# Moving accumulating DMAs of block sums, and operands at a pair's border, in an attention and feed-forward kernel

## The chip, the cores and the metric

The kernel runs on one core of a Trainium2 chip. The core has a matrix engine (TensorE, in the profile PE, with its weight loads as PEld), a vector engine (VectorE, DVE), a scalar engine (ScalarE, ACT) and GpSimd (POOL). SyncE (SP), ScalarE and GpSimd issue DMAs from queues of their own. Each engine works through its instructions in the order in which they were planned. The metric is the time of one execution on the device in microseconds (us); lower is better.

## The reference, cut to what matters

Attention within chunks of 64 tokens, whose result is the input of a feed-forward network with a leaky activation:

```python
scores = scale * np.matmul(q_c, k_c.transpose(0, 1, 2, 4, 3))      # 8 batches, 8 heads, chunks of 64, head size 64
scores = scores - np.max(scores, axis=-1, keepdims=True)
attn = np.exp(scores)
attn = attn / (np.sum(attn, axis=-1, keepdims=True) + 1e-09)
x = np.matmul(attn, v_c)                    # 4608 tokens x 512, once the heads are side by side
h = x @ w_in                                # 512 x 2048
g = np.maximum(h, 0.0) + alpha * np.minimum(h, 0.0)
out = g @ w_out                             # 2048 x 512
```

All is float32. The kernel keeps that precision on TensorE by splitting each operand into a high and a low part (`hi`, `lo`) and adding three products: high by high, low by high and high by low.

## The kernel before

The 4608 tokens are 36 pieces of 128 (`NSUB`) and 9 blocks of 512. The first three blocks (`PLAIN`) go through the network directly. The other six go in three pairs; a pair's two products are done by a scheme with seven half-size products in place of eight (`ORDERS` holds the order of the seven), for which combinations of weights are needed.

**The plain blocks.** There are 48 steps (`n`, from 0). Step `n` takes 128 of the 2048 hidden features (`f`) of one block: an input product of 12 matmuls into a bank of `ps_h` (`ffn_in`, L318), PReLU on ScalarE and VectorE (`prelu`, L308 to L310), a split (L330, L331), and an output product of 12 matmuls into the four banks `ps_o` (`ffn_out`, L343). The output product comes one step later, and from step 20 on two steps later (`pending`). Blocks 0 and 1 are done in two turns each (`phases`, `TURNS`), since the weights are still arriving: features 0 to 2 of block 0, 0 to 8 of block 1, then the rest of each, then all of block 2. After a first turn `store` copies the four banks to SBUF and stores them in DRAM tiles `partial` (L375). After the second turn it copies them to `more` (rows 0 and 1, one tile with one buffer), to `ob` (row 2) and to `g` (row 3) at L372, and adds each in DRAM to its `partial` with an accumulating DMA from GpSimd's queue (L377). Block 0's second turn ends in step 26 and block 1's in step 33. SyncE moves the sums from `partial` to the output in step 47 (L774).

**Combinations of weights.** In the sixteen steps of `COMBINE` (20, 22, 23, 24, 26, 29, 30, 31, 33, 35, 36, 37, 39, 40, 41, 43) `combine` takes a pair of weight tiles, forms sums and differences on VectorE (L499 to L509), splits two results with a cast on ScalarE (L515) and a subtraction on VectorE (L516), and stores each in two halves from GpSimd's queue (L477). The split tiles are buffers of a stage pool: `raw` has two buffers, `more` one. With `early`, only `raw` is used; otherwise the three take turns.

**Attention beside it.** From step 21 on, pieces of attention are done by visits between the matmuls (`visit`, at the half steps of `visits`): values of an older piece (L279) and scores of a new one (L201) into two banks `ps_a`, then maxima on VectorE (L217), exponentials on ScalarE (L221), sums and a transposition (L223 to L232, eight small DMAs at L239), and copies of the older piece's result (L295, L304, L305). The next visit uses the same two banks. Since `pinned` is set from step 20 on, TensorE's order is the program's; the other engines' orders are written by a planner that simulates the kernel in time and goes by priorities (`high_priority`, offset 300) and by `issue_after`, which puts an instruction behind another one on the same engine.

**The pairs.** A pair has eight rounds of `first_product` (L598: input products and PReLU, with tiles `gh`, `g` and `gl` of two buffers each), and then `second_product` (L714): seven products of eight operands each, numbered 0 to 55 (`at`), each six matmuls long. An operand is split by `operand` (L554 and L555), two operands ahead of its use (`AHEAD`), into tiles that go by `at % 4`: 0 into the two buffers `t1`, 1 into `more`, 2 and 3 into `gh` and `gl`. The combined weights stream in from GpSimd's queue (L536). At the end of the last pair `add` adds the last two banks to `y21` (L676), and `done` stores the two results from SyncE's queue (L685).

Of the kernel before, what the change touches and what calls it, by code (L numbers as in the profile page):

```python
# [27 lines left out]
def tile_local_attention_prelu_ffn(  # L28
# [12 lines left out]
    nc = tc.nc  # L41
# [31 lines left out]
    def f32(t):  # L73
        return t.bitcast(F32)
# [272 lines left out]

    partial = {}
    finals = []

    def store(acc, b, keep):
        for t, o in enumerate(acc):
            rows = slice(b * TB + t * P, b * TB + (t + 1) * P)
            before = partial.get((b, t))
            if b == PLAIN - 1:
                ob = const.tile([P, DM], F32, name=f"wi{NF - 2 - t}")
            elif keep and b == 0:
                side = "wi" if t % 2 else "wo"
                ob = const.tile([P, DM], F32, name=f"{side}{NF - 1 - t // 2}")
            elif keep:  # L360
                pool, name = ((load, "q_sb"), (load, "v_sb"), (load, "v_sb"), (soft, "pr"))[t]
                ob = pool.tile([P, DM], F32, name=name, bufs=2 if name == "v_sb" else 1)
            elif t < 2:
                if t == 0:
                    both = stage.tile([P, 2, DM], F32, name="more", bufs=1)
                ob = both[:, t]
            elif t == 2:
                ob = stage.tile([P, DM], F32, name="ob", bufs=1)
            else:
                ob = gp.tile([P, DM], F32, name="g")  # L370
            with tc.high_priority(offset=HIGH):
                nc.scalar.copy(ob, o)  # L372
            if keep:
                partial[b, t] = dram.tile([P, DM], F32, name=f"partial{b}_{t}")
                nc.sync.dma_start(out=partial[b, t], in_=ob)  # L375
            elif before is not None:
                nc.gpsimd.dma_start(out=before, in_=ob, accum_op=ALU.add)  # L377
                finals.append((out[rows, :], before))
            else:
                nc.sync.dma_start(out=out[rows, :], in_=ob)  # L380
# [93 lines left out]

    def keep_a(side, i, j, a):
        n, u = unit(side, i, j)
        nc.gpsimd.dma_start(out=units[side][n][:, u], in_=f32(a))  # L477

    halves = (slice(0, 2 * P), slice(2 * P, 4 * P))

# [10 lines left out]
    def combine(side, j, early):  # L491

        ws = wi if side == "wi" else wo
        pair = [ws[j], ws[JF + j]]
        left, right = halves
        a = []
        for w in pair:
            t = stage.tile([P, 512], F32, name="t1")
            nc.vector.tensor_tensor(t, f32(w[:, 0]), f32(w[:, 1]), op=ALU.add)  # L499
            a.append(t)  # L500
        a11, a22 = a[0][:, left], a[1][:, right]
        if side == "wi":
            a12, a21 = a[0][:, right], a[1][:, left]
        else:
            a21, a12 = a[0][:, right], a[1][:, left]
        nc.vector.tensor_tensor(a22, a21, a22, op=ALU.add)
        nc.vector.tensor_tensor(a21, a11, a21, op=ALU.subtract)
        nc.vector.tensor_tensor(a11, a22, a11, op=ALU.subtract)
        nc.vector.tensor_tensor(a12, a12, a11, op=ALU.subtract)  # L509
        names = ((2, 4), (3, 1)) if side == "wi" else ((2, 3), (4, 1))  # L510
        for t, name in zip(a, names):
            which = "raw" if early else ("raw", "raw", "more")[fetched[0] % 3]
            fetched[0] += 1
            w = stage.tile([P, 2, 512], F32R, name=which, bufs=2 if which == "raw" else 1)
            nc.scalar.copy(w[:, 0], t)  # L515
            nc.vector.tensor_tensor(w[:, 1], t, f32(w[:, 0]), op=ALU.subtract)  # L516
            for half, s in zip((left, right), name):
                keep_a(side, {1: 5, 2: 6, 3: 7, 4: 3}[s], j, w[:, :, half])

    sequence = [(side, n) for _ in range(NPAIR) for side in ("wi", "wo") for n in range(7 * JF // 2)]  # L520
    ring = []
# [130 lines left out]
    def operand(g, at):  # L652
        i, j = ORDERS["wo"][at // JF], at % JF
        b11, b12, b21, b22 = pieces(g, j)
        if i == 7:
            t = gp.tile([P, TB], F32, name="g")
            with tc.issue_after(behind[0][1].ins):
                nc.vector.tensor_tensor(t, b22, b12, op=ALU.subtract)
        else:
            t = {1: b11, 3: b22, 2: b21}.get(i, b12)  # L660
        if at % 4 == 1:
            both = stage.tile([P, 2, TB], F32R, name="more", bufs=1)
            hi, lo = both[:, 0], both[:, 1]
        else:
            pool, names = (stage, ("t1", "t1")) if at % 4 == 0 else (gp, ("gh", "gl"))
            hi, lo = (pool.tile([P, TB], F32R, name=name) for name in names)
        behind[:] = behind[1:] + [split(t, hi, lo)]
        return hi, lo

    def second_product(g, b, operands, conversion, end):  # L670
# [3 lines left out]
        def add(ys, ps):  # L674
            for m in range(2):
                nc.vector.tensor_tensor(ys[:, m], ps[m], ys[:, m], op=ALU.add)  # L676

        def copy(ys, ps):
            for m in range(2):
# [15 lines left out]
        for i in ORDERS["wo"]:  # L695
            if i == 6:
                ps = kept
            else:
                if i in (5, 4):
                    turn[0] += 2  # L700
                ps = [bank() for _ in range(2)]
            if i == 1:
                kept = ps
            for j in range(JF):
                at = JF * ORDERS["wo"].index(i) + j
                if at + AHEAD + EARLIER < 7 * JF:
                    difference(g, at + AHEAD + EARLIER)
                if at + AHEAD < 7 * JF:
                    operands.append(operand(g, at + AHEAD))
                hi, lo = operands.pop(0)  # L710
                w = weight("wo", i, j)
                for m in range(2):
                    for n, (l, xx) in enumerate(((0, hi), (0, lo), (1, hi))):
                        pe(nc.tensor.matmul(  # L714
                            ps[m], lhsT=w[:, l, m * P:(m + 1) * P], rhs=xx,
                            start=i != 6 and j == 0 and n == 0, stop=j == JF - 1 and n == 2,
                            skip_group_check=i == 6,
                        ))
                if (i, j) in sums:
                    to, what, m = sums[i, j]  # L720
                    op = {} if to is y22 and what is y21 else {"accum_op": ALU.add}
                    with tc.issue_after(streamed[0].ins):
                        nc.gpsimd.dma_start(out=to[:, m], in_=what[:, m], **op)
                    if what is y11 and to is not y21:
                        done(to, m, *((1, 1) if to is y22 else (0, 1)))
                if conversion and j % 4 == 3:
                    with tc.issue_after(behind[1][0].ins), tc.issue_after(behind[1][1].ins):
                        conversion.pop(0)()
            if i == 1:
                copy(y11, ps)  # L730
            elif i == 7:
                copy(y21, ps)
            elif i == 2:
                add(y11, ps)
                for m in range(2):
                    done(y11, m, 0, 0)
            elif i == 5:
                copy(y12, ps)
            elif i == 3:
                add(y12, ps)  # L740
            elif i == 6:
                copy(y11, ps)
            else:
                add(y21, ps)
                for m in range(2):
                    done(y21, m, 1, 0)
# [8 lines left out]
    for n, (p, b, f) in enumerate(steps):  # L755
# [25 lines left out]
        if ready < NF:  # L781
            prepare(ready, done_x.get({2: SPB, 3: SPB + 2, 4: SPB + 3}.get(ready)))
            ready += 1
        elif n in COMBINE:

            with tc.issue_after(stages["softmax"][0].ins), tc.issue_after(stages["softmax"][1].ins):
                combine(*combined.pop(0), n in (23, 24, 25, 26, 32, 33, 34))
        if n == len(steps) - 8:
            ops, conversion = convert(PLAIN)
        if len(steps) - 8 <= n < len(steps) - 4:  # L790
# [21 lines left out]
    for pair in range(NPAIR):  # L812
        b = PLAIN + 2 * pair
        more = pair + 1 < NPAIR
        if more:
            new_raw(b + 2)
        g = {}
        for j in range(JF):
            if more:
                new += 1  # L820
                visit(new - 2, new if new < NSUB else None)
            if j == JF - 1:
                operands = [operand(g, at) for at in range(AHEAD)]
            first_product(ops, g, j)
        if more:
            ops, conversion = convert(b + 2)
        second_product(g, b, operands, conversion, not more)
# [39 lines left out]
```

## Time and profile before

| what | value |
| --- | --- |
| median of three runs | 847.34 us |
| lowest and highest run | 846.77 and 848.85 us |
| profiled execution, its time | 848.08 us |
| profiled execution, its span | 846.3 us |
| mean granted clock of TensorE | 0.988 |
| DMA traffic | 192.40 MB, mean 227 GB/s |

The span goes from the first to the last instruction of the profiled execution; its time has some 1.8 us around that. In the views of the profile a row of the order of time has its start, its duration (both in us), engine, line, operation, output and inputs, shapes and how many were merged; in brackets stands how long the engine was idle before it and what ended that. "L343" is line 343 of the kernel. A row of waits has who waited, for whom, the total in us, how often, and the longest. A row of windows has the stretch, its length, the busy time of PE, PEld, DVE, ACT and POOL with their instructions, the granted clock of TensorE, the share of the DMA engines and GB/s. A row of DMA issues has the median time from issue to landing.

### The profile page before, as it was taken

Reading aid. Unit: us, or ns where it says so; the run is one execution under the profiler, and the core shown is the slowest. Engines: PE = TensorE matmul, PEld = TensorE weight load, DVE = VectorE, ACT = ScalarE, POOL = GpSimd, SP = SyncE. Lnnn points to the kernel's source line nnn. Section 1 sums busy time; section 2 is a strip of 40 time slices with the busy share of each in tenths; the row PEclk is TensorE's granted clock in tenths of the full one; section 3 lists DMA queues with packets and bytes.
Section 4 is the critical chain, followed back from the end, with each engine's and each line's share of the span. In section 5 each row is a group of like instructions: output and inputs, shape, how many; then the busy total and the mean of one; then the engine's idle time right before and its main releaser. Section 6 shows DMA issues by size and latency. Waiting matters only on the chain.

```text
span 846.3 us, 15382 instructions
## 1 busy us (share of the span) xinstructions
PE 808.6 (96%) x5248; PEld 646.1 (76%) x5248; DVE 670.9 (79%) x1267; ACT 545.5 (64%) x1392; POOL 213.0 (25%) x339
## 2 busy tenths in 40 slices
PE   4699999999798999999989999999999999999998
PEld 4567888777576778777767877777887888888886
DVE  5798999978797987676778997676789966568875
ACT  6976676656666767678775564877766546556552
POOL 3006222224244331111111242111122421112232
PEclk8999999999899999999999999999999999999999
DMA  9729787558678667687774789876567995555778
GB/s 274 212 76 332 242 257 262 175 169 214 192 234 225 203 215 259 215 259 258 255 260 149 242 221 326 276 253 225 175 209 234 240 310 181 192 186 188 244 218 236
DMA packets 74942, 192.40 MB, mean 227 GB/s; under 512 B 11888, under 2 KB 19056, under 8 KB 74736
## 3 DMA queue, kind: packets, MB, share of 16 engines
q0 software_dynamic: 38240, 127.42, 47.7%
q1 hardware_dynamic: 28480, 49.44, 18.5%
q10 hardware_dynamic: 8144, 14.56, 5.5%
q8 instruction: 42, 0.69, 0.3%
q14 instruction: 36, 0.29, 0.1%
HBM read 135.27 MB, written 42.99 MB: 211 GB/s over the span
## 4 chain that ended last, share of the span: by engine, by line
PE 66%; ACT 9%; DMA 9%; DVE 8%; SPq 4%; issue 3%; ACTq 0%; DVEq 0%; POOL 0%
PE ps_o L714 15%; PE ps_o L598 12%; PE ps_h L714 12%; PE ps_o L343 9%; PE ps_h L318 9%; PE ps_h L598 6%; SPq L239 4%; DMA pT<-t 4%; ACT pr L221 3%; DVE t L232 1%; DMA wi_a<-raw 1%; DMA v_sb<-v 1%; DMA more<-w_in 1%; PE ps_a L279 1%; DVE raw L516 1%
## 5 line engine op out<-in xcount | busy, mean ns | idle before, releaser
L343 PE MATMUL ps_o<-wo,gh 128*128 128x512 f32 x384 | 115.2, 396 | 3.2 <-ACT more L372 3.2
L318 PE MATMUL ps_h<-xh,wi 128*128 128x512 f32 x384 | 106.6, 402 | 3.0 <-DVE g L310 2.3
L318 PEld LDWEIGHTS ps_h<-xh,wi 128*128 128x128 f32 x384 | 71.9, 190 | 21.0 <-DVE g L310 2.9
L343 PEld LDWEIGHTS ps_o<-wo,gh 128*128 128x128 f32 x384 | 71.6, 188 | 20.9 <-ACT more L372 3.6
L221 ACT ACTIVATE pr<-ps_a,mx 128x64 f32<-128x64 f32 x224 | 67.2, 327 | 30.2 <-DVE mx L218 22.8
L343 PE MATMUL ps_o<-wo,gl 128*128 128x512 f32 x192 | 69.8, 395 | 0.0
L598 PE MATMUL ps_o<-wi,raw 128*128 128x512 f32 x171 | 67.9, 397 | 0.0
L598 PE MATMUL ps_o<-wo,raw 128*128 128x512 f32 x171 | 67.8, 396 | 0.0
L318 PE MATMUL ps_h<-xl,wi 128*128 128x512 f32 x192 | 54.0, 400 | 0.0
L221 ACT ACTIVATION_READ_ACCUMULATOR pr<-ps_a,mx 128x1 f32 x224 | 49.3, 220 | 0.0
L554 ACT CAST gh<-wi 128x512 fp32r<-128x512 f32 x48 | 29.9, 623 | 29.4 <-PE ps_o L714 15.1
L308 ACT ACTIVATE wo<-gh 128x512 f32<-128x512 f32 x24 | 15.2, 634 | 51.5 <-DVE gh L621 51.5
L536 POOL DMA_DIRECT2D raw<-wi_a x42 | 22.4, 532 | 103.0 <-PE ps_o L598 61.6
L536 POOL DMA_DIRECT2D raw<-wo_a x42 | 22.3, 532 | 91.9 <-PE ps_o L714 48.6
L318 PEld LDWEIGHTS ps_h<-xl,wi 128*128 128x128 f32 x192 | 36.6, 191 | 8.8
L330 ACT CAST gh<-g 128x512 fp32r<-128x512 f32 x48 | 29.8, 622 | 20.4 <-DVE g L310 15.3
L343 PEld LDWEIGHTS ps_o<-wo,gl 128*128 128x128 f32 x192 | 36.1, 188 | 8.7
L598 PE MATMUL ps_o<-wi,wo 128*128 128x512 f32 x99 | 39.3, 397 | 0.0
L598 PE MATMUL ps_o<-wo,wo 128*128 128x512 f32 x99 | 39.1, 395 | 0.0
L308 ACT ACTIVATE g<-ps_h 128x512 f32<-128x512 f32 x48 | 29.5, 614 | 13.9 <-PE ps_h L318 13.6
L598 PEld LDWEIGHTS ps_o<-wo,raw 128*128 128x128 f32 x171 | 32.2, 188 | 7.7
L598 PEld LDWEIGHTS ps_o<-wi,raw 128*128 128x128 f32 x171 | 32.1, 188 | 7.6
(242 smaller groups left out, 2281.5 us busy)
## 6 DMA issues: line engine op xcount, KB each, us to landing
raw<-wi_a POOLq DMA_DIRECT2D x42, 512.0 KB, 4.8
raw<-wo_a POOLq DMA_DIRECT2D x42, 512.0 KB, 4.5
wi<-wi_a POOLq DMA_DIRECT2D x21, 512.0 KB, 4.9
wo<-wi_a POOLq DMA_DIRECT2D x21, 512.0 KB, 4.6
wi<-wo_a POOLq DMA_DIRECT2D x21, 512.0 KB, 4.1
wo<-wo_a POOLq DMA_DIRECT2D x21, 512.0 KB, 4.2
v_sb<-v SPq DMA_DIRECT2D x28, 256.0 KB, 5.1
pT<-t SPq DMA_DIRECT2D x224, 32.0 KB, 3.7
```

The lines of the kernel that those rows point to most:

```text
L221: last = nc.scalar.activation(pr[:, g], one, AF.Exp, bias=mx[:, g], scale=SCALE, accum_out=sm[:, g])
L232: nc.vector.transpose(tb.rearrange("p j h t -> p h j t"), pr)
L239: nc.sync.dma_start(out=pT[dst, i].rearrange("p h t -> p (h t)"), in_=tb[src, j].rearrange("p h t -> p (h t)"),)
L279: pe(nc.tensor.matmul(att[c][par * C:(par + 1) * C, hp * C:(hp + 1) * C], lhsT=v_sb[rows, h * C:(h + 1) * C], rhs=p[rows, :, par * NP + hp ...
L308: nc.scalar.activation(g, h, AF.Relu, scale=-1.0)
L318: pe(nc.tensor.matmul(hps, lhsT=wi[f][:, l, k * P:(k + 1) * P], rhs=xx[:, k], start=(i == 0 and k == 0), stop=(i == 2 and k == NK - 1),))
L330: nc.scalar.copy(gh, g)
L343: pe(nc.tensor.matmul(o, lhsT=a[:, ts], rhs=wo[f][:, l], start=(f == first and i == 0), stop=(f == last and i == 2),))
L536: streamed[0] = nc.gpsimd.dma_start(out=f32(t), in_=units[side][n])
L554: hi = nc.scalar.copy(t_hi, t)
L598: pe(nc.tensor.matmul(ps, lhsT=w[:, l, k * P:(k + 1) * P], rhs=xx[:, xl], start=first and at == 0, stop=at == n - 1, skip_group_check=not ...
L714: pe(nc.tensor.matmul(ps[m], lhsT=w[:, l, m * P:(m + 1) * P], rhs=xx, start=i != 6 and j == 0 and n == 0, stop=j == JF - 1 and n == 2, ski ...
```

## The change

It has four parts.

- Of the four accumulating DMAs at the end of a second turn, those of rows 0 to 2 are put on a list (`adds`) and not issued by `store`. `combine` takes one from the list after each of its two results and issues it behind that result's second store. The one of row 3 stays where it was.
- In steps 23 to 36 all combinations use the two buffers of `raw` alone. Before, this held for steps 23, 24, 26 and 33 among those that combine.
- Around a pair's border three operands are made ahead of the last `first_product` in place of two. Operand 2 goes into `gh` and `ob`, operand 3 into two buffers of `g`. Operands 3 and 4 are made one step sooner and at a priority of 600; at operand 2 none is made, and then it goes on two ahead.
- The last addition of the last pair is done in two halves of columns; each result is stored at once, and the very last half from ScalarE's queue.

```diff
@@ def store
             elif before is not None:
-                nc.gpsimd.dma_start(out=before, in_=ob, accum_op=ALU.add)
+                if t < 3:
+                    adds.append((before, ob))
+                else:
+                    nc.gpsimd.dma_start(out=before, in_=ob, accum_op=ALU.add)
                 finals.append((out[rows, :], before))
@@ def keep_a
-        nc.gpsimd.dma_start(out=units[side][n][:, u], in_=f32(a))
+        return nc.gpsimd.dma_start(out=units[side][n][:, u], in_=f32(a))
@@ def combine
             for half, s in zip((left, right), name):
-                keep_a(side, {1: 5, 2: 6, 3: 7, 4: 3}[s], j, w[:, :, half])
+                stored = keep_a(side, {1: 5, 2: 6, 3: 7, 4: 3}[s], j, w[:, :, half])
+            if adds:
+                to, what = adds.pop(0)
+                with tc.issue_after(stored.ins):
+                    nc.gpsimd.dma_start(out=to, in_=what, accum_op=ALU.add)
@@ def operand
-        if at % 4 == 1:
+        if at == 2:
+            hi, lo = gp.tile([P, TB], F32R, name="gh"), stage.tile([P, TB], F32R, name="ob", bufs=1)
+        elif at == 3:
+            hi, lo = (gp.tile([P, TB], F32R, name="g") for _ in range(2))
+        elif at % 4 == 1:
@@ def second_product
+        def finish(ys, ps):
+
+            for m in range(2):
+                for part in ((slice(0, TB),) if m == 0 else (slice(0, TB // 2), slice(TB // 2, TB))):
+                    nc.vector.tensor_tensor(ys[:, m, part], ps[m][:, part], ys[:, m, part], op=ALU.add)
+                    rows = slice((2 + m) * P, (3 + m) * P)
+                    first = (b - PLAIN) * TB
+                    queue = nc.scalar if part.start else nc.sync
+                    queue.dma_start(out=outT[rows, first + part.start:first + part.stop], in_=ys[:, m, part])
...
-                if at + AHEAD < 7 * JF:
-                    operands.append(operand(g, at + AHEAD))
+
+                ahead = at + AHEAD + (at < 2)
+                if at != 2 and ahead < 7 * JF:
+                    with tc.high_priority(offset=2 * HIGH) if at < 2 else nullcontext():
+                        operands.append(operand(g, ahead))
...
+            elif end:
+                finish(y21, ps)
@@ the steps
-                combine(*combined.pop(0), n in (23, 24, 25, 26, 32, 33, 34))
+                combine(*combined.pop(0), 23 <= n <= 36)
@@ the pairs
-                operands = [operand(g, at) for at in range(AHEAD)]
+                operands = [operand(g, at) for at in range(AHEAD + 1)]
```

More of the change, by code (lines that the diff above doesn't have):

```diff
@@ L349, in tile_local_attention_prelu_ffn @@
     finals = []
+    adds = []
     def store(acc, b, keep):
```

## The prediction

> **What bounds the kernel now.** I read the page first (how busy TensorE is), then the waits of TensorE, then the order of time around each wait.
>
> ```profile
> span 846.3 us, 15382 instructions
> PE 808.6 (96%) x5248; PEld 646.1 (76%) x5248; DVE 670.9 (79%) x1267; ACT 545.5 (64%) x1392; POOL 213.0 (25%) x339
> PE ps_a L279 <- issue: 4.7, 1, 4.7
> PE ps_o L343 <- ACT more L372: 3.2, 1, 3.2
> PE ps_o L714 <- DVE gl L555: 2.8, 3, 2.5
> PE ps_h L318 <- DVE g L310: 2.3, 2, 1.6
> ```
>
> TensorE is busy for 96% of the span, and the change takes no matmul away: it can gain only what TensorE loses in waits, and what it loses just behind them. Three single waits (4.7, 3.2 and 2.5 us) stand at the places that the change touches. The first, with TensorE's rows and the granted clock (the figure before the DMA share):
>
> ```profile
> 197.00 0.69 PE L279 MATMUL ps_a<-pT,v_sb 64*64 64x64 f32 x32
> 200.99 0.63 PE L343 MATMUL ps_o<-wo,gh 128*128 128x512 f32 x2
> ...
> 216.04 0.40 PE L343 MATMUL ps_o<-wo,gl 128*128 128x512 f32 x1
> 221.17 0.31 PE L279 MATMUL ps_a<-pT,v_sb 64*64 64x64 f32 x2 [4.73 <-issue]
> ...
> 228.78 0.63 PE L343 MATMUL ps_o<-wo,gh 128*128 128x512 f32 x2
> ...
> 224.00:228.10 4.10, 4.10 (x13) 3.22 (x11) 4.07 (x10) 0.95 (x4) 1.79 (x3) 0.50 0.85 233
> 257.10:261.00 3.90, 3.90 (x76) 3.10 (x76) 2.31 (x4) 2.24 (x4) 3.90 (x6) 1.00 0.91 231
> 443.10:446.60 3.50, 3.50 (x8) 2.37 (x9) 3.20 (x6) 1.93 (x4) 0.00 (x0) 0.51 0.19 69
> ```
>
> An undisturbed visit, from its first matmul (197.00) to the next output matmul (200.99), takes 3.99 us. The disturbed one was due at 216.04 + 0.23 = 216.27 (matmuls of an undisturbed run start 0.23 us apart: 48 in 11.05 us in a row below), so 228.78 should have been 220.26. The loss is **8.5 us**: 4.9 of waiting, the rest a visit and an input product at a granted clock of 0.5. What held it:
>
> ```profile
> 197.30 0.93 POOL L377 DMA_DIRECT2D partial<-ob  x1 [1.60 <-ACT ob L372]
> 202.46 3.10 POOL L477 DMA_DIRECT2D wi_a<-raw  x4 [0.67 <-DVE raw L516]
> ...
> 210.36 0.62 ACT L515 CAST raw<-t 128x512 fp32r<-128x512 f32 x1 [3.17 <-DMA wi_a<-raw]
> 213.09 0.62 ACT L515 CAST raw<-t 128x512 fp32r<-128x512 f32 x1 [2.11 <-DMA wi_a<-raw]
> 213.61 0.59 ACT L308 ACTIVATE g<-ps_h 128x512 f32<-128x512 f32 x1
> ...
> 220.69 0.37 DVE L305 TENSOR_TENSOR xl<-ps_a,xh 128x256 fp32r<-128x256 f32 x1
> ...
> wi_a<-raw POOLq DMA_DIRECT2D x4, 256.0 KB, 7.1
> wi_a<-raw POOLq DMA_DIRECT2D x4, 256.0 KB, 3.1
> ```
>
> Block 0's four accumulating DMAs leave GpSimd's queue in one burst (197 to 202), and four stores of a combination behind it. These land after 7.1 us; those of the next combination (issued 212 to 216) after 3.1. ScalarE, in order, stands before the two casts until buffers of `raw` are free, so its PReLU for an input product that TensorE had long finished waits till 213.61. VectorE follows, and the last reader of the visit's `ps_a` (L305) starts at 220.69, just ahead of TensorE's 221.17. So this wait, put down to "issue", is the burst's.
>
> The second wait and the third:
>
> ```profile
> 241.20 1.45 POOL L477 DMA_DIRECT2D wi_a<-raw  x2 [4.88 <-DVE mx L218]
> 247.66 1.45 POOL L477 DMA_DIRECT2D wi_a<-raw  x2 [3.57 <-DVE raw L516]
> 249.10 1.45 POOL L477 DMA_DIRECT2D wi_a<-more  x2
> ...
> 255.31 1.21 ACT L515 CAST raw<-t 128x512 fp32r<-128x512 f32 x2
> 256.35 1.15 ACT L372 COPY more<-ps_o 128x512 f32<-128x512 f32 x2
> 257.06 0.73 PE L343 MATMUL ps_o<-wo,gh 128*128 128x512 f32 x2 [3.18 <-ACT more L372]
> ...
> 437.54 1.28 DVE L630 TENSOR_TENSOR gl<-ps_h,g 128x512 f32<-128x512 f32 x2
> 441.15 0.69 DVE L310 SCALAR_TENSOR_TENSOR wi<-gl,wi 128x512 f32<-128x512 f32 x1 [0.92 <-ACT wi L309]
> 442.36 0.68 DVE L555 TENSOR_TENSOR gl<-wi,gh 128x512 fp32r<-128x512 f32 x1
> ...
> 437.40 1.55 PE L714 MATMUL ps_o<-t,raw 128*128 128x512 f32 x6
> 443.10 0.73 PE L714 MATMUL ps_o<-gl,raw 128*128 128x512 f32 x1 [2.54 <-DVE gl L555]
> ...
> 453.24 11.07 PE ps_h L714 x48
> 608.28 1.55 PE L714 MATMUL ps_o<-t,raw 128*128 128x512 f32 x6
> 619.54 11.05 PE ps_h L714 x48
> ```
>
> At the end of block 1, rows 0 and 1 are copied into `more`. A combination had stored from that tile at 249.10; the copies come at 256.35, behind two casts, and TensorE gets its bank 3.18 us late. At the first pair's border, the third operand's low half needs a buffer of `gl`, both held by PReLU's inputs until L310 at 441.15. From 437.40 to 453.24 the first 48 matmuls take 15.84 us; in pair 1, from 608.28 to 619.54, they take 11.26. The loss is **4.6 us**: 2.5 of waiting, the rest at a clock of 0.51. Pairs 1 and 2 lose nothing there.
>
> **The change part by part.**
>
> *Six of eight accumulating DMAs move.* Nothing is removed: the same 256 KB each, 0.93 us of POOL's issue. They move past later stores of combinations on POOL's queue; that is busy for 25%, and waited 1.60 us for the copy ahead of the first of them. The add of row 3 stays and waits only for its own copy. Block 0's others follow steps 29 (two) and 30, block 1's steps 35 (two) and 36; the final stores read the sums in step 47, which hides their later landing. An add waits for its copy and for the first turn's store, both long done, so nothing queues behind it. What goes: the stores issued at 202.46 stand behind one add, not four. At 3.1 instead of 7.1 us, the second cast runs 4.0 us sooner, and what is behind it on ScalarE and VectorE too: TensorE would start at 221.17 - 4.0 = 217.2 against 216.3 due. I leave **0.8 us** (bounds 0, as the planner may order the casts later, and 4.9, the whole wait), without the slow clock. Gain 8.5 - 0.8 = **7.7**.
>
> *Two buffers in steps 29 to 36.* With `more` left to the adds, block 1's copies find it free: the adds follow step 29's stores, those before 241.20, two combinations ahead of the store at 249.10 that holds the tile now. Gain **3.2** (bounds 0 and 3.2).
>
> *What it adds.* Four adds cost the stores behind them 4.0 us, 1.0 each. Two adds may stand between the stores of one combination and the cast that waits for its buffer: 2.0 us of ScalarE, with exponentials and PReLU queued behind the cast and TensorE's next visit waiting for those. In combinations 30, 31, 35 and 36 (29 used `raw` twice already) the third buffer no longer covers this. Stores of neighbouring combinations start 6.5 us apart (241.20, 247.66), while 3.1 + 2.0 = 5.1 suffices, so mostly it is covered. I take **1.5 us** in all; bounds 0 and 8.5, one stop like that of 221.
>
> *Border operands.* Operand 2 uses a second `gh` and the idle `ob`, and is made before the last first product. Operand 3 uses two `g`, whose last reader, L630, ends at 438.82; TensorE needs it at 437.40 + 3 x 1.4 = 441.6, and its cast and subtraction take 0.62 and 0.68 (as at 210.36 and 442.36). No instruction is added, only ScalarE's and VectorE's order changes: two casts pass PReLU steps, which delays operand 7 by 2 x 0.62 = 1.2 us, and that is not due before 437.40 + 7 x 1.4 = 447.2. I leave 0.4 us (bounds 0 and 4.6): gain **4.2**, in pair 0 alone.
>
> *The end.*
>
> ```profile
> 841.51 1.40 DVE L676 TENSOR_TENSOR xh<-ps_h,xh 128x512 f32<-128x512 f32 x2 [3.55 <-PE ps_h L714]
> 842.23 1.03 SPq L685 DMA_DIRECT2D outT<-xh  x2
> L506 DVE TENSOR_TENSOR t<-t,t 128x256 f32<-128x256 f32 x8 | 3.4, 422 | 0.2
> ...
> pT<-t SPq DMA_DIRECT2D x224, 32.0 KB, 3.7
> ```
>
> The last addition (0.69) becomes two of some 0.42 (L506, the nearest half), so the last store starts 0.15 us later, with half the bytes, on ScalarE's empty queue. From the last issue (843.3) to the end lie 3.0 us; were all of that bytes, half would go, -1.5 + 0.15. But 32 KB take 3.7 us elsewhere, so the bytes are little of it. I take -0.3, near that row (bounds -1.35 and +0.15).
>
> **Sum**, against the profiled execution's own 848.08 (span 846.3 and 1.8 around it): 848.1 - 7.7 - 3.2 - 4.2 - 0.3 + 1.5 = 834.2. That execution lies 0.74 above the median of the runs shown, 847.34; so **833.4 us**.
>
> The half clock is weighed once more. It stood at 0.51 behind the wait of 2.54 us, but at 1.00 around the longer one of 3.18, so how long an idle time brings it is not settled by these rows; I give it back with both waits. The Trainium skill ("TensorE: Matmul & The Clock Gate", Part 1) halves the clock only after an idle window of about 3.4 us; by that the 2.54 us at the border would not be its cause, and the sum 1.7 us more. The first wait agrees with it, the border's does not.
>
> **The rivals.**
>
> *The slow clock at the border is not the wait's* (the rule above). For it: 3.18 us passed without. Against: the 0.51 begins with the wait's end. Half of 3.5 us stays: 835.1.
>
> *One stop returns.* In the new order a cast waits for a landing behind adds, as at 210.36, and TensorE stops once as at 221. For it: VectorE is 79% busy, and the visit keeps no slack (217.2 against 216.3). Against: at most two adds stand together. 833.4 + 8.5 = 841.9. The Trainium skill speaks for it ("DMA: Bandwidth & Descriptors", Issuing engines are not separate DMA queues): all transfers share the same engines, so a moved add still takes its turn there. The 7.1 against 3.1 us agrees.
>
> *The border stays.* The planner sets the splits behind PReLU as before: 833.4 + 4.2 = 837.6. Against: their priority is raised, and L630 ends early.
>
> *It doesn't do what it says.* The planner writes each engine's order anew; if its casts and copies land as late, TensorE waits as now and gains only the end: 847.
>
> *Slower.* Two-buffer combinations wait for their own stores. The point from which it decides is a landing later than the 6.5 us between neighbours (7.1 was seen behind four adds). Then each costs 8.5; two of the four give 833.4 + 17 = 850.4, a third more. Against: 5.1 is expected.
>
> **How the numbers follow.** Forecast 0.55, slow clock 0.08, one stop 0.17, border 0.07, nothing gained 0.07, slower 0.06. A measurement of this kernel tells about 0.3% (2.5 us) from no change, so faster is 0.87, same 0.07, slower 0.06. The range starts at 829: no new waits (-1.5), nothing left at visit and border (-1.2), and the wait of 1.6 us of L318 gone too. It ends at 843, one stop and a little. Outside lie the last two cases (0.13) and the ends of the others, about 0.2.
>
> **What would show it.** Right: no burst of L377; stores behind it landing near 3 us; no TensorE wait over 1 us between 216 and 260; the first pair's 48 matmuls near 11.2 us; a clock of 1.0 throughout. Wrong: L515 waiting for stores in steps 30 to 37, visits with new waits (L279), or TensorE's wait at L714 as before.

## The result and the profile after

The changed kernel takes 841.52 us (median of six executions, 840.06 to 842.27); the kernel before, measured beside it on the same chip, 848.45 (846.77 to 849.96). The ratio is 0.9909, with an interval from 0.9886 to 0.9931: faster by 0.7 to 1.1%. Faster was forecast, and the range of 829 to 843 holds the time. The forecast itself, 833.4, is 8.1 us too low: of 13.9 us, half came (6.9 between the medians). The rival "one stop returns" had been priced at 841.9.

The head of the page after, against 846.3 us and nearly the same PE time (808.6) before:

```profile
span 840.5 us, 15376 instructions
PE 808.1 (96%) x5248; PEld 646.3 (77%) x5248; DVE 669.8 (80%) x1268; ACT 544.2 (65%) x1392; POOL 214.0 (25%) x339
```

**Where the time went, stretch by stretch.** TensorE executes the same 3168 large matmuls (128 x 512) in the same order in every kernel of this study, so the starts of the 660th, 720th, 828th, 936th, 1032nd, 1404th and 1512th (counted from 0) cut the span into stretches that can be compared, whatever the clock time. The starts are read off the order of time of TensorE; the lengths are their differences.

| stretch | what lies in it | before, us | after, us | difference |
| --- | --- | --- | --- | --- |
| to 660 | weights arriving, blocks 0 and 1 | 207.77 | 209.26 | +1.5 |
| 660 to 720 | the visit at 221 | 23.81 | 16.85 | -7.0 |
| 720 to 828 | with the end of block 1, near 255 | 32.45 | 32.82 | +0.4 |
| 828 to 936 | block 2, up to 290 | 29.76 | 34.57 | +4.8 |
| 936 to 1032 | block 2, up to 320 | 26.98 | 26.50 | -0.5 |
| 1032 to 1404 | block 2's rest, pair 0's first products | 95.67 | 95.66 | 0.0 |
| 1404 to 1512 | the border in pair 0 | 31.04 | 26.46 | -4.6 |
| 1512 to 3168 | the rest of the pairs | 394.29 | 393.70 | -0.6 |
| last matmul to end | the last stores | 4.52 | 4.68 | +0.2 |

Two stops went about as forecast (-7.0 and -4.6). Block 1's end gave nothing in sum, and 4.8 us came back at a place that had no stop before. The longest waits of TensorE between 195 and 330 us after (who waited for whom, the total, how often, the longest), to be held against the 4.7 and 3.2 shown of before:

```profile
PE ps_a L279 <- ACT xl L295: 2.1, 1, 2.1
PE ps_o L343 <- ACT g L373: 1.3, 1, 1.3
PE ps_a L279 <- DVE raw L520: 1.3, 1, 1.3
PE ps_a L279 <- DMA pT<-t: 0.8, 1, 0.8
```

Order of time after, GpSimd and TensorE around the visit at 221 and block 1's end (L381 is the add issued at once, L481 the store of a combination, L526 the deferred add):

```profile
199.80 0.94 POOL L381 DMA_DIRECT2D partial<-g  x1 [2.72 <-ACT g L373]
202.90 2.18 POOL L481 DMA_DIRECT2D wi_a<-raw  x3 [2.17 <-DVE raw L520]
...
218.38 0.29 PE L279 MATMUL ps_a<-pT,v_sb 64*64 64x64 f32 x2 [0.45 <-issue]
219.32 0.63 PE L279 MATMUL ps_a<-pT,v_sb 64*64 64x64 f32 x27 [0.64 <-DVE xl L305]
...
253.47 0.73 PE L343 MATMUL ps_o<-wo,gh 128*128 128x512 f32 x2 [1.31 <-ACT g L373]
...
256.39 2.90 POOL L481 DMA_DIRECT2D wi_a<-raw  x4 [1.74 <-DVE raw L520]
```

and the DMA issues of after between 202 and 206.4 us (KB each, us to landing), where before 7.1 stood:

```profile
wi_a<-raw POOLq DMA_DIRECT2D x4, 256.0 KB, 4.9
```

The burst is gone, one add stands ahead of the stores, and of the 4.73 us of waiting ahead of the visit 0.45 are left; the 0.64 behind its first matmuls stood there before, too (0.63). At block 1's end the bank comes 1.31 us late, not 3.18. But the combination of step 31, whose stores before went out at 247.66 and 249.10, ahead of block 1's end, now stores at 256.39, behind it. And a new stop stands in the next stretch. Order of time after, rows chosen from four engines:

```profile
274.24 1.45 POOL L481 DMA_DIRECT2D wo_a<-raw  x2 [3.85 <-DVE mx L218]
275.68 0.95 POOL L526 DMA_DIRECT2D partial<-more  x1
276.27 1.82 POOL L481 DMA_DIRECT2D wo_a<-raw  x2
277.71 1.35 POOL L526 DMA_DIRECT2D partial<-more  x1
...
283.17 0.62 ACT L519 CAST raw<-t 128x512 fp32r<-128x512 f32 x1 [2.45 <-DMA wo_a<-raw]
283.82 0.69 DVE L520 TENSOR_TENSOR raw<-t,raw 128x512 fp32r<-128x512 f32 x1 [1.17 <-ACT raw L519]
285.04 0.75 DVE L217 TENSOR_REDUCE mx<-ps_a 128x4 f32<-128x256 f32 x2
287.10 0.31 ACT L221 ACTIVATE pr<-ps_a,mx 128x64 f32<-128x64 f32 x1
289.42 0.68 ACT L295 COPY xl<-ps_a 128x256 f32<-128x256 f32 x2
289.88 0.41 PE L279 MATMUL ps_a<-pT,v_sb 64*64 64x64 f32 x2 [2.12 <-ACT xl L295]
291.59 1.02 PE L279 MATMUL ps_a<-pT,v_sb 64*64 64x64 f32 x27 [1.30 <-DVE raw L520]
```

It is the old stop in a new place. ScalarE stands 2.45 us before a cast until a buffer of `raw` is free, whose stores went out between two adds. VectorE's subtraction and the maxima of the visit come behind it, the eight exponentials behind these, and the copy that frees `ps_a` (L295) last; TensorE's next visit waits 2.12 us for it, and 1.30 us more behind its first matmuls, which the view puts down to VectorE's subtraction. Then the clock is at half. Windows of after:

```profile
289.90:296.90 7.00, 5.70 (x72) 4.75 (x73) 5.32 (x11) 3.08 (x6) 2.89 (x4) 0.51 0.56 184
436.60:447.70 11.10, 11.10 (x49) 9.02 (x48) 10.11 (x17) 9.15 (x17) 2.12 (x4) 1.00 0.66 222
```

The second row is the border. The chain that ended last, between 430 and 450 us, has there

```profile
436.78 11.09 PE ps_o L739 x48
```

which answers to the 15.84 us of before: no wait, and a clock of 1.00.

### The profile page after: what moved, and what is told of

The parts are those of the page before. It is cut to its first block, busy times and chain, and to the rows that moved or that the text cites. A ratio compares the mean times of both kernels' runs of the same rounds, so it can differ in the third digit from the quotient of the medians.

```text
span 840.5 us, 15376 instructions
## 1 busy us (share of the span) xinstructions
PE 808.1 (96%) x5248; PEld 646.3 (77%) x5248; DVE 669.8 (80%) x1268; ACT 544.2 (65%) x1392; POOL 214.0 (25%) x339
## 4 chain that ended last, share of the span: by engine, by line
PE 78%; DMA 7%; ACT 5%; DVE 5%; SPq 2%; issue 2%; POOL 1%; ACTq 0%; DVEq 0%; POOLq 0%
PE ps_o L606 19%; PE ps_o L739 15%; PE ps_h L739 12%; PE ps_h L318 10%; PE ps_o L343 10%; PE ps_h L606 9%; SPq L239 2%; PE ps_a L279 1%; DMA pT<-t 1%; ACT pr L221 1%; DMA more<-w_out 1%; PE ps_a L201 1%; DMA more<-w_in 1%; DMA wo_a<-raw 1%; DVE raw L520 1%
## 5 line engine op out<-in xcount | busy, mean ns | idle before, releaser
L330 ACT CAST gh<-g 128x512 fp32r<-128x512 f32 x48 | 29.8, 622 | 25.9 <-DVE g L310 23.6
L562 ACT CAST gh<-wi 128x512 fp32r<-128x512 f32 x45 | 28.1, 624 | 25.2 <-PE ps_o L739 11.0
L331 DVE TENSOR_TENSOR gl<-g,gh 128x512 fp32r<-128x512 f32 x48 | 32.7, 682 | 4.8 <-ACT gh L330 4.4
```

Source lines behind the costliest of these rows:

```text
L330: nc.scalar.copy(gh, g)
L331: low = nc.vector.tensor_tensor(gl, g, f32(gh), op=ALU.subtract)
L562: hi = nc.scalar.copy(t_hi, t)
```

## The experiments

Short diffs are against the changed kernel, unless another is named. All ratios are to the kernel before on the same chip, with their interval. Lengths of stretches are those of one profiled execution each; a table at the end puts them side by side. Two of these executions were slower than all others of their kernel: 844.43 us against 838.89 to 839.39 (three buffers in steps 30, 31 and 36) and 844.44 against 841.25 to 842.34 (without block 1's late adds).

**The border alone.**

```diff
@@ store: all adds at once, as before; the end as before
@@ the steps
-                combine(*combined.pop(0), 23 <= n <= 36)
+                combine(*combined.pop(0), n in (23, 24, 25, 26, 32, 33, 34))
```

> The kernel before with the operands at the pair's border alone (three ahead, operands 2 and 3 in gh, ob and g, raised priority). Theory: the border's wait and its half clock go, 4.6 us faster than before (843.5 to 844.2), the first 48 matmuls of the first pair's second product take 11.1 us in place of 15.8, and TensorE's waits of 4.7 and 3.2 us near 221 and 257 stay. Rival (the planner's new order elsewhere gave the gain): within 1 us of before.

Measured: 845.15 us, ratio 0.9944 [0.9923, 0.9965]. The border's stretch has 26.5 us, as in the changed kernel, and TensorE waits at the old places from 195 to 330 us (4.7 and 3.2 before):

```profile
PE ps_o L343 <- ACT more L373: 3.7, 1, 3.7
PE ps_a L279 <- issue: 3.0, 1, 3.0
```

What follows: the border part is worth 4.6 us in its stretch by itself, as much as together with the rest.

**The adds and the buffers alone**, with the border and the end of before (the blocks of the diff in `operand`, `second_product` and the pairs taken back).

> The kernel before with the deferred adds and the two-buffer combinations alone; border and end as before. Theory: the gain near 221 and 257 (about 8 us) is given back near 290 by the new stop (about 6 us), so 1 to 3 us faster than before, with the border's 2.5 us wait in place. Rival (adds and border hang together through the planner's order): no stop near 290, and 8 us faster.

Measured: 845.34 us, ratio 0.995 [0.9925, 0.9975]. The stretch at 221 falls to 16.3 us, and the new stop is there too, for the transposed exponentials this time, 3.3 us in the longest; waits of TensorE, 195 to 330 us:

```profile
PE ps_a L279 <- DMA pT<-t: 4.8, 3, 3.3
```

What follows: the new stop belongs to the adds and the buffers, as the theory had it, though 4.8 us were gained between the medians and not 1 to 3. These two parts together are worth about as much as the border (0.9950 and 0.9944), not the 9.4 us net of the forecast.

**Without block 1's late adds.** The kernel leaves the sums of rows 0 to 2 of block 1 out.

```diff
-                    adds.append((before, ob))
+                    adds.append((before, ob)) if b == 0 else None
```

> The changed kernel without the three deferred adds of block 1 (rows 0 to 2 of that block stay at their first turn's part); buffers as in the changed kernel. Theory: the stop of 2.1 and 1.3 us near 290 with its half clock comes from the stores that stand behind these adds (landing 6.1 us); it goes, and the time is 5 to 6 us under the changed kernel, near 836. Rival (the two raw buffers are the cause whatever stands between): the stop stays and the time is within 1.5 us of the changed kernel.

Measured: 841.86 us, ratio 0.9915 [0.9885, 0.9945]: no faster than the changed kernel, a miss. TensorE in order of time:

```profile
290.19 0.94 PE L279 MATMUL ps_a<-pT,v_sb 64*64 64x64 f32 x29 [1.19 <-ACT xl L295]
...
316.08 0.95 PE L279 MATMUL ps_a<-pT,v_sb 64*64 64x64 f32 x29 [2.40 <-ACT xl L295]
```

From 230 to 330 us no cast of a combination waits for the landing of a store any more, and the stop at 290 shrinks to 1.19 us, but one of 2.40 us stands one visit later. What follows: the late adds set the size of the stop at 290, but are not all of its cause. With the adds away the visits still run late, by the same chain from the exponentials to L295.

**Before, without the burst** (diff against the kernel before; the sums of rows 0 to 2 of block 0 are left out).

```diff
-                nc.gpsimd.dma_start(out=before, in_=ob, accum_op=ALU.add)
+                if b or t == 3:
+                    nc.gpsimd.dma_start(out=before, in_=ob, accum_op=ALU.add)
```

> The kernel before without the accumulating DMAs of rows 0 to 2 of block 0 (those rows stay at their first turn's part). Theory: the burst makes the wait of 4.7 us near 221; without it the stores behind land after about 3 us, the wait falls under 1.5 us, its half clock goes, and the time is 6 to 7.5 us under before. Rival (the planned order of VectorE and ScalarE makes it): a wait over 3 us stays near 221, within 2 us of before.

Measured: 843.77 us, ratio 0.9939 [0.9904, 0.9973]. The stretch at 221 has 16.0 us against 23.8, so the burst was that stop. But block 1's end now loses more than before (38.4 us against 32.4); the wait of TensorE there:

```profile
PE ps_o L343 <- ACT more L372: 5.6, 1, 5.6
```

What follows: 7.8 us won at one place, 6.0 given back at the next. The stop at 221 had delayed TensorE, and so hidden how late the copies into `more` are: they start at 253.18 here and at 256.35 before, 3.2 us sooner, and TensorE is there 5.6 us sooner. ScalarE is not idle just ahead of them in either; the exponentials, L295 and two casts stand before them in its order.

**Three buffers in steps 30, 31 and 36.**

```diff
-                combine(*combined.pop(0), 23 <= n <= 36)
+                combine(*combined.pop(0), 23 <= n <= 35 and n not in (30, 31))
```

> The changed kernel, but the combinations of steps 30, 31 and 36 use all three buffers again (29 and 35 stay on two). Theory A (two buffers push the combinations from step 31 on past the end of block 1, where they bunch up and meet block 1's adds): step 31's stores come ahead of block 1's end again, the stretch of matmuls 828 to 936 falls from 34.6 to 31 us or less, and the time is 3 to 5 us under the changed kernel. Theory B (the adds themselves make the stop near 290): the stop stays, within 1.5 us of the changed kernel.

Measured: 839.35 us, ratio 0.9909 [0.9876, 0.9943]. The stop at 290 is gone (28.9 us for its stretch), and block 1's end has one of 6.2. Order of time:

```profile
250.34 1.46 POOL L481 DMA_DIRECT2D wi_a<-more  x2 [3.38 <-DVE mx L218]
...
255.97 1.16 ACT L373 COPY more<-ps_o 128x512 f32<-128x512 f32 x2
256.69 1.22 PE L343 MATMUL ps_o<-wo,gh 128*128 128x512 f32 x2 [6.21 <-ACT more L373]
```

What follows: with the third buffer in step 31, its stores from `more` start at 250.34, and the copies of block 1 come after them. That wait is what the two buffers remove. Theory A is right about the stores and the stretch at 290, but not about the time: the ratio is the changed kernel's, and in its profile the 5.7 us won from 828 to 936 are lost as 7.0 at block 1's end.

**One add for each combination**, behind the last of its four stores.

```diff
-            if adds:
-                to, what = adds.pop(0)
-                with tc.issue_after(stored.ins):
-                    nc.gpsimd.dma_start(out=to, in_=what, accum_op=ALU.add)
+        if adds:
+            to, what = adds.pop(0)
+            with tc.issue_after(stored.ins):
+                nc.gpsimd.dma_start(out=to, in_=what, accum_op=ALU.add)
```

> The changed kernel, but one add per combination, behind its last store (steps 29, 30, 31 and 35, 36, 37), so that no add stands between the two results of a combination. Theory B: fewer bytes ahead of a store, the stop near 290 is halved, 2 to 3 us under the changed kernel. Theory A: the bunching stays, within 1.5 us of it.

Measured: 856.19 us, ratio 1.0079 [1.0044, 1.0113], slower than the kernel before. Waits of TensorE, 195 to 330 us:

```profile
PE ps_o L343 <- ACT ob L373: 12.2, 1, 12.2
PE ps_o L343 <- ACT more L373: 5.5, 1, 5.5
```

What follows, as neither text had it: block 0's adds now end as late as step 31, and block 1's copies need the same tiles `more` and `ob`. In the changed kernel the last add from `more` follows step 29 and that from `ob` step 30; one combination later was too late for both: ScalarE stands 4.00 us before the copy into `more` and 1.66 us before that into `ob` until the add from that tile has landed. A deferral has a latest date, set by the next user of the tile that it reads.

**Block 0's adds deferred, with block 1's at once and the buffers of before.**

```diff
-                if t < 3:
+                if t < 3 and b == 0:
...
-                combine(*combined.pop(0), 23 <= n <= 36)
+                combine(*combined.pop(0), n in (23, 24, 25, 26, 32, 33, 34))
```

> The changed kernel, but only block 0's rows 0 to 2 are deferred; block 1 adds at once as before, and the combinations use the buffers of the kernel before (two in 23 to 26 and 32 to 34). Theory A: the 7 us near 221 stay gained, nothing bunches near 290, 4 to 6 us under the changed kernel. Rival: the block end of block 1 costs 3 to 6 us again (copy into more late), within 1.5 us of the changed kernel or over it.

Measured: 841.51 us, ratio 0.9926 [0.9904, 0.9948], about the changed kernel's, as the rival had it. 15.8 us for the stretch at 221, and at block 1's end

```profile
PE ps_o L343 <- ACT more L373: 7.1, 1, 7.1
```

**Two buffers alone**, all adds at once.

```diff
-                if t < 3:
+                if False:
```

> The changed kernel with all adds at once as before (no deferral), but with the two buffers in steps 23 to 36. Against the kernel with the border's part alone. Theory A: the two buffers alone push step 31's combination behind block 1's end and make the stretch of matmuls 828 to 936 3 to 5 us longer (29.0 there). Theory B: that stretch stays within 1.5 us of 29.0.

Measured: 845.04 us, ratio 0.9967 [0.9948, 0.9986]. Waits of TensorE, 195 to 330 us:

```profile
PE ps_a L279 <- ACT xl L295: 3.8, 2, 2.1
PE ps_a L279 <- issue: 2.9, 1, 2.9
```

What follows from these two: block 1's end is mended by the two buffers alone (no wait on L373 is left, 29.5 us for the stretch), not by the deferral; the stop at 221 is mended by the deferral alone. And the buffers have their own price, without any late add: stops of 2.08 us at 290.13 and 1.76 us at 315.93, behind L295. Step 31's stores go out behind block 1's end here too (256.32); the stretch 828 to 936 has 31.5 us against 29.0, so 2.5 more, less than theory A and more than theory B had.

**Two buffers up to step 34, block 1's adds at once.**

```diff
-                if t < 3:
+                if t < 3 and b == 0:
...
-                combine(*combined.pop(0), 23 <= n <= 36)
+                combine(*combined.pop(0), 23 <= n <= 34)
```

> The changed kernel with block 1's second-turn results added at once again, and two buffers in steps 23 to 34 only (35 and 36 use all three). Theory (the burst makes the stop at 221, the third buffer in step 31 makes the wait at block 1's end, and the late adds with the two-buffer steps 35 and 36 make the stop at 290): 221 free of a stop (its stretch 16 us), no wait of PE on the copies of block 1 near 254 (the stretch of pair 0's start to 286 about 29.5 to 33 us), no wait on a DMA of wo_a near 283; 660th to 1032nd large matmul in 106 to 108 us and 836 to 838 us in all. Rival (VectorE and ScalarE have no slack, each stop removed comes back at the next visit): stops of 1.8 to 2.1 us on the softmax's results near 290 and 316 as in the kernel with two buffers only, 109 to 111 us for the stretch, 840 to 842 us in all.

Measured: 843.78 us, ratio 0.9938 [0.9911, 0.9964]: slower than either text said, though the three stops of the theory are small or gone. TensorE in order of time:

```profile
254.60 0.73 PE L343 MATMUL ps_o<-wo,gh 128*128 128x512 f32 x2 [1.48 <-ACT g L373]
...
315.98 0.95 PE L279 MATMUL ps_a<-pT,v_sb 64*64 64x64 f32 x29 [2.40 <-ACT xl L295]
```

The stop at 290 went, and the one at 316 came back with 2.40 us, as the rival had it.

**The same, with step 30 on three buffers** (diff against the run just above).

```diff
-                combine(*combined.pop(0), 23 <= n <= 34)
+                combine(*combined.pop(0), 23 <= n <= 34 and n != 30)
```

> As the one before it, but step 30's combination on all three buffers, so that step 31's can start sooner and less of the work is bunched behind block 1's end. Theory: step 30's stores from the third buffer land before block 1's end, so the copies do not wait; step 31's stores go out before 253 and not at 256; the stops at 290 and 316 shrink; 835 to 838 us. Rival (the third buffer decides whichever step uses it): the wait on block 1's copies near 254 is back with 3 to 6 us and the half clock behind it, 840 to 842 us.

Measured: 839.78 us, ratio 0.9887 [0.9843, 0.9932]. Waits of TensorE, 195 to 330 us:

```profile
PE ps_a L279 <- ACT xl L295: 2.5, 2, 2.1
PE ps_o L343 <- ACT more L373: 1.3, 1, 1.3
```

What follows: neither text is met in full. Block 1's copies hardly wait, but step 31's stores start at 254.40, still behind block 1's end, and a wait of 2.07 us stays at 286.89, without the half clock. From the 660th to the 1032nd matmul it is the shortest of all, 107.5 us against 110.7. Its ratio isn't clear of the changed kernel's, so it is the best guess for a next version and not shown to be one.

**Three buffers in steps 30 and 36, and the changed kernel once more**, both on one chip.

```diff
-                combine(*combined.pop(0), 23 <= n <= 36)
+                combine(*combined.pop(0), 23 <= n <= 35 and n != 30)
```

> The changed kernel, all six adds deferred, with three buffers in steps 30 and 36 and two in between. Theory (the third buffer hurts in step 31 alone, since only its stores are still under way when block 1 ends; at 290 the two buffers of step 36 make the casts wait for the landing of stores behind late adds): a wait of at most 1.5 us on block 1's copies near 248 to 254, none above 1 us near 287 to 290, no half clock from 216 to 300; 660th to 1032nd large matmul in 105 to 107 us; 835 to 838 us. Rival (the side engines have no slack and a removed stop comes back): a stop of 2 us or more on the softmax's results between 280 and 320, 107.5 us or more for the stretch, 839 to 842 us, the same as the run with block 1's adds at once.

> The changed kernel once more, unchanged, on the same chip as the run with three buffers in steps 30 and 36, so that the two can be told apart. Theory: 841 to 842 us, 0.990 to 0.992 of the kernel before, the stop of 2.1 and 1.3 us near 290 again, and 3 to 6 us more than the other kernel. Rival: within 2 us of the other kernel.

Measured: 841.0 us, ratio 0.9923 [0.9897, 0.9948], and for the changed kernel 841.41 us, ratio 0.9909 [0.9878, 0.994]. Waits of TensorE from 216 to 330 us, first of the one with three buffers in 30 and 36:

```profile
PE ps_a L279 <- DMA pT<-t: 3.8, 3, 2.5
```

then of the changed kernel:

```profile
PE ps_a L279 <- DMA pT<-t: 3.1, 1, 3.1
PE ps_a L279 <- ACT xl L295: 1.3, 1, 1.3
```

What follows: the two can't be told apart, as the rival said. The third buffer in step 36 doesn't remove the stop at 290 when step 31 comes late; in the run with three buffers in 30, 31 and 36 it was absent because TensorE had just stood 6.2 us at block 1's end, and the other engines had caught up (argued from the order of time; not tried by itself). The changed kernel's stretches repeat within 0.4 us. Those of the kernel before and of the border alone, whose work stands in the same order on ScalarE, VectorE and GpSimd from the 660th to the 1032nd matmul, differ by 0.8 to 2.0 us each and by 1.0 in the sum; some 1.4 of the 2.0 us is the half clock, which followed the wait at block 1's end in one and not in the other. So a difference of 2 us in one stretch shows nothing by itself.

**All runs side by side**, stretches in us:

| kernel | ratio | 660 to 720 | 720 to 828 | 828 to 936 | 936 to 1032 | 660 to 1032 | border |
| --- | --- | --- | --- | --- | --- | --- | --- |
| before | 1 | 23.8 | 32.4 | 29.8 | 27.0 | 113.0 | 31.0 |
| border alone | 0.9944 | 22.0 | 34.4 | 29.0 | 28.6 | 114.0 | 26.5 |
| two buffers alone (and border) | 0.9967 | 21.9 | 29.5 | 31.5 | 28.7 | 111.6 | 26.5 |
| block 0 deferred, old buffers (and border) | 0.9926 | 15.8 | 39.0 | 29.2 | 26.6 | 110.7 | 26.5 |
| changed | 0.9909 | 16.8 | 32.8 | 34.6 | 26.5 | 110.7 | 26.5 |
| changed, once more | 0.9909 | 17.0 | 32.7 | 34.5 | 26.8 | 111.1 | 26.5 |
| adds and buffers alone | 0.9950 | 16.3 | 33.2 | 34.6 | 27.0 | 111.0 | 29.8 |
| without block 1's late adds | 0.9915 | 15.9 | 35.0 | 30.5 | 30.4 | 111.7 | 26.5 |
| before without the burst | 0.9939 | 16.0 | 38.4 | 29.1 | 25.2 | 108.7 | 29.5 |
| three in 30, 31, 36 | 0.9909 | 16.9 | 39.8 | 28.9 | 25.8 | 111.5 | 26.8 |
| one add each | 1.0079 | 16.3 | 50.4 | 32.8 | 25.5 | 125.0 | 26.5 |
| two up to 34 | 0.9938 | 16.1 | 35.4 | 29.5 | 28.7 | 109.7 | 26.5 |
| two up to 34, not in 30 | 0.9887 | 16.1 | 33.9 | 31.4 | 26.1 | 107.5 | 26.5 |
| three in 30 and 36 | 0.9923 | 16.4 | 32.5 | 33.8 | 26.7 | 109.3 | 26.5 |

Read the rows "border alone", "two buffers alone", "block 0 deferred" and "changed" together. The buffers win 4.9 us at block 1's end (34.4 to 29.5) and 2.4 in the sum. The deferral wins 6.2 at 221 (22.0 to 15.8) and 3.3 in the sum. Both together, in the changed kernel, win 3.3 (114.0 to 110.7) and not 5.7: either eats what the other wins. The times of the executions don't show the buffers' gain: two buffers alone have 0.9967 and the border alone 0.9944, with overlapping intervals. Of all these kernels only two buffers alone and the one with one add each are clear of the changed kernel, and both are slower.

## Why the prediction was right, and where it failed

**The visit at 221** (7.7 of 8.5 us): right. 7.0 measured, with 0.45 us left of the wait where 0.8 was allowed, and the second wait of 0.6 as before. The stores landed after 4.9 us, not 3.1. That the burst was the cause is shown by the kernel before without it (16.0 us for the stretch). Since TensorE's wait was put down to "issue" there, the cause had to be read from ScalarE's rows, and that reading held.

**Block 1's end** (3.2): the mechanism was right and incomplete. With `more` free, the copies come in time; two buffers alone leave no wait on them. What was missing is that the time depends on when TensorE gets there: the kernels that mend 221 and keep step 31's third buffer wait 5.6 to 7.1 us there. In the changed kernel TensorE's bank is still 1.31 us late, and waits of 0.80, 0.30 and 0.20 us stand in the stretch that it did not have before, so it gains nothing (+0.4).

**What it adds** (1.5, bounds 0 and 8.5): this step failed. It compared a landing of 5.1 us with combinations 6.5 us apart and called the rest covered. But the distance of 6.5 us was taken from the kernel before, where the third buffer lets step 31's casts run ahead of block 1's end. With two buffers its stores go out 8.7 us later (256.39 against 247.66), behind block 1's copies and a visit's exponentials, and the visits behind have nothing to spare. That the two buffers alone do this is shown by the run with all adds at once (stores at 256.32, stops at 290 and 316); that the late adds make the stop at 290 as large as it is, by the run without them. The stretch to 290 lost 4.8 us, within the bounds and three times the value taken.

**The border** (4.2): right, 4.6 in its stretch, no wait left, and the same when done alone. The slow clock left with the wait, so the rival that kept 1.7 us of it fell; why it had followed this wait and not the longer one is told at the end.

**The end** (-0.3): not found. From the last matmul to the end lie 4.52 us before and 4.68 after; over all runs, 4.5 to 4.9 with the old end and 4.5 to 5.1 with the new one.

**The sum.** Of -13.9 us forecast, the profiled executions show -5.8 (846.3 to 840.5). By the table of stretches, measured less forecast: +0.7 at 221 (-7.0 against -7.7); +6.4 from block 1's end to 320 (+4.7 in three stretches against -3.2 and +1.5); -0.4 at the border; +0.5 at the end; +0.9 elsewhere (+1.5 ahead of the 660th matmul, -0.6 in the pairs). That makes the 8.1. The +1.5 at the start is no work of the change: the 660th matmul starts anywhere from 206.85 to 210.56 us in these fourteen profiles.

**The rivals.** "One stop returns" is what happened, even by its mechanism in the changed kernel: a cast that waits for a landing behind adds (2.45 us at 283.17). It was given 0.17 because "at most two adds stand together". The runs show why that was no protection: with all adds at once, or block 1's left out, a stop returns as well, at 290 or 316, by the visit's own chain. What deserved more weight was the argument for it that stands there, that a visit keeps no slack. That its number, 841.9, is met within 0.4 us is luck: the stop cost 4.8 us and not 8.5, and block 1's end and the start make up for it. The range holds the time because it was drawn to take in this rival; of the forecast itself, the signs are mixed. The burst is gone and the 48 matmuls take 11.09 us, but the stores land after 4.9 us and not near 3, TensorE waits 1.31 us at 253.47, and the clock falls to half near 290; and two of the three signs of being wrong are there, a cast of step 36 that waits 2.45 us for stores and a visit with a new wait of 2.12 us. "Slower" didn't occur in the change; the same tiles' reuse makes it so in the kernel with one add each.

**What stays open.** An edit can make the planner write the orders of ScalarE, VectorE and GpSimd anew, and a stop returns in nearly every version between 250 and 320 us. In some pairs of runs the order is not the reason. From the 660th to the 1032nd matmul the kernel before has the same order of work on all three engines as without the burst, and yet 6.0 of 7.8 us came back; two buffers alone and the run without late adds have the same on ScalarE and VectorE, and the stops at 290 and 316 are 2.08 and 1.76 us in one, 1.19 and 2.40 in the other. For the changed kernel against the kernel before, where the orders differ, it stays open how much is the engines' load (VectorE 80% of the span) and how much the order.

## What to carry to other kernels

When side engines feed a bound engine without slack, a stop removed is a delay removed for the bound engine only: ask what it meets sooner, at the next block end and the next visit, and give the gain back until a row shows room there. A distance between two steps, taken from the profile of before, isn't valid once the buffers that made it are taken away. And a deferred read of a buffer has a date: the next writer of that buffer, which may be the same code one block later.

## What the runs showed of the hardware

The half clock doesn't follow from the length of a wait between 2 and 4 us. Before, it followed the wait of 2.54 us at the border and not the one of 3.18 at block 1's end; behind waits of 2.08 us (two buffers alone, 290.13) and 2.07 us (step 30 on three, 286.89) it came in the first and not in the second. It also counts where the wait lies. In each of the fourteen traces the granted clock changes only at moments that are whole multiples of 3.41 us apart; before, at 221.33, 228.15, 443.19 and 446.61 among others. Windows of before cut along this grid (the third figure is PE's busy time, the figure before the DMA share the clock), two around the wait of 3.18 us and two around that of 2.54:

```profile
252.05:255.46 3.41, 1.83 (x8) 1.12 (x6) 1.75 (x6) 3.41 (x19) 1.07 (x2) 1.00 1.10 263
255.46:258.87 3.41, 1.81 (x8) 1.50 (x9) 2.47 (x4) 3.26 (x7) 1.84 (x3) 1.00 0.96 236
439.78:443.19 3.41, 0.87 (x5) 0.41 (x3) 2.49 (x5) 3.41 (x7) 0.53 (x1) 1.00 0.81 257
443.19:446.61 3.42, 3.42 (x8) 2.29 (x9) 3.12 (x6) 1.84 (x4) 0.00 (x0) 0.50 0.18 67
```

The longer wait is cut in two, and both stretches keep 1.8 us of matmuls; the shorter one lies in one stretch, which keeps 0.87, and the next runs at half. Cut like this from 100 to 830 us, every stretch at full clock with 1.5 us of matmuls or less is followed by one at half, in all fourteen traces, and none with 1.94 us or more is; between these both occur.

The Trainium skill ("TensorE: Matmul & The Clock Gate", Part 1) says that the clock's window runs freely, so that the moment of a change depends on where in the window the work falls; the grid of 3.41 us agrees. It also asks for an idle window of about 3.4 us, and the half clock behind a stretch with 0.87 us of matmuls shows that a partly busy one can do; the measurement decides.
